# Chunk attention in units of two groups of tokens, and the values of an expert pair as one planned step

## The chip, the cores and the metric

One core of a Trainium2 chip runs the kernel. The metric is device time in microseconds (us), the median of several runs; lower is better. TensorE (PE in the profile) multiplies matrices into PSUM, which has 8 banks of 128 partitions by 512 floats; VectorE (DVE), ScalarE (ACT) and GpSimd (POOL) work on what stands there and in SBUF; SyncE (SP) only issues transfers.

## The reference, cut to what matters

```python
# q, k, v: batch 8, heads 8, sequence 576, head dimension 64
# 1. attention inside chunks of 64 tokens, per head
attn = softmax(q_c @ k_c.T / 8)              # 64 x 64 per chunk and head
x = (attn @ v_c)                             # -> x: 8 x 576 x 512
# 2. four attention experts over x, the two best of them per token
w = softmax over the 2 largest of x @ w_gate
for e in range(4):
    q, k, v = x @ wq[e], x @ wk[e], x @ wv[e]        # 64 wide
    a = softmax(causal(q @ k.T / 8))                 # 576 x 576
    out += (token chose e) * w * ((a @ v) @ wo[e])
```

## The kernel before

The 8 x 576 tokens are cut into 36 groups of 128 tokens (two chunks, all eight heads), g = 0 to 35; four and a half groups make one batch element. Two kinds of work are mixed all along the program.

The **chunk stage** (`stage_a`) takes one group per call. Keys and queries come by DMA into `ks` and `qs`, values into `vs` (256 KB each, three tiles of each kind). TensorE multiplies the scores of 64x64 blocks into two banks (L353, 256 columns of each used). VectorE takes the maximum per bank (L362) and subtracts it (L364), ScalarE takes the exponential (L367), VectorE sums (L369; a 65th column of `e` holds the reference's epsilon) and inverts (L371), and GpSimd multiplies `e` by the inverse into a further tile `en` (L373). TensorE transposes `en` into two banks (L383), ScalarE copies them to `et` (L387), TensorE multiplies with the values (L402), and ScalarE and VectorE write the result as a high and a low part, `xh` and `xl` (L420, L422), which are two fp32r numbers for one fp32.

The **expert stage** runs per batch element: projections of queries and keys for pairs of experts (L451, three products of high and low parts each), values and gate logits (L327), scores (L543), softmax (L553, L561), weights with the gate (L583), transposes (L616, L629 and, on VectorE, L594), values (L648: `values` works on one pair of experts, in two parts of 128 and 448 columns, each with a bank of its own), and the output projection (L676).

What sets the order is a **planner** that runs while the program is built. Every step is added with an engine, a duration, what it depends on, the buffers that it uses, and a key (from the table `KEYS`). `emit` walks through modelled time: whenever an engine is free, the ready step with the lowest key is written out, if its buffers are free. The engines then execute those lists in that fixed order. Each TensorE step has a *form*, after how it splits the array: `full` (128 rows by 128 columns: projections, values and logits, output), `rows` (64 rows by 128 columns: transposes and scores), `cols` (128 by 64: values) and `quarters` (64 by 64: the chunk stage's two products, and the expert scores of the first 64 queries). A step whose form differs from the step before costs `CHANGE` more in the model, and among ready steps whose keys lie within `KEYS["same"]` of the best one of the present form is preferred:

```python
if eng == "PE":
    dur = pe_time(dur + (CHANGE if got.form != form else 0.0), got.share, now)
    form = got.form
```

While TensorE has nothing ready in the first 25 us of modelled time, `emit` writes fillers there, bf16 products of a tile `warm` (L711), to keep the array occupied.

Of the kernel before, what the change touches and what calls it, by code (L numbers as in the profile page):

```python
# [22 lines left out]
NI = 5  # L23
W_VG = E * D + E
# [17 lines left out]
CHANGE = 0.12  # L42
# [13 lines left out]
class Plan:  # L56
# [26 lines left out]
    def emit(self, fill, until):  # L83
# [21 lines left out]
        while left:  # L105
            for eng, heap in avail.items():
# [3 lines left out]
                while heap:  # L110
# [58 lines left out]
def dve_t(n):  # L169
    return 0.075 + 1.04e-3 * n  # L170
# [6 lines left out]
def pool_t(n):  # L177
# [3 lines left out]
KEYS = dict(lead=0.362, a_tr=-3.09, a_av=0.234, a_x=3.312, v=-1.218, vx=2.515, gate=-3.755, q0=1.309, k0=0.512,  # L181
            q1=-0.208, k1=0.186, s0=0.821, s1=1.869, s2=0.46, s3=-0.308, p_soft=0.779, p_tr=0.357, av0=1.956,
            av1=1.843, wo=3.522, vl=5.664, l_qk=8.956, l_v=0.845, l_o=1.057, w=2.854, same=0.118, f_q0=-1.052,
            f_k0=-0.783, f_q1=2.257, f_k1=-1.57, f_v=-0.37, f_vx=3.133, f_gate=1.333, f_s0=0.013, f_s2=-0.982,
            f_av0=0.066, f_av1=0.054, z_q0=-0.132, z_k0=-1.251, z_q1=0.635, z_k1=0.769, z_v=-0.784, z_gate=3.547,
            z_s0=-0.408, z_s2=0.264, z_av0=-1.381, z_av1=0.48, z_wo=1.518, h0=2.856, h1=-0.163, h2=0.071, h3=-0.324)
# [12 lines left out]
def chunked_attention_then_attention_experts(ctx: ExitStack, tc: tile.TileContext, qt, kt, vt, wqk, wvg, wo, out):  # L199
# [12 lines left out]
    q_p = tiles(3, [128, HP, 128], "qs")  # L212
    k_p = tiles(3, [128, HP, 128], "ks")
    vs_p = tiles(3, [128, H, D], "vs")
    e_p = tiles(3, [128, H, 65], "e")
    en_p = tiles(2, [128, DM], "en")
    et_p = tiles(3, [128, 2, 256], "et")
    xc_p = list(zip(tiles(1, [128, KT, 128], "xch", F32R), tiles(1, [128, KT, 128], "xcl", F32R)))
    mx_p = tiles(6, [128, 3, H, 1], "mx")
# [15 lines left out]
    for e in e_p:  # L235
        pool.memset(e[:, :, 64:65], EPS)
# [27 lines left out]
    def load(g):  # L264
        q_s[g], k_s[g], vs_s[g] = Slot(q_p), Slot(k_p), Slot(vs_p)

        def f():
            nc.sync.dma_start(k_s[g].t, kt[g])
            (nc.sync if g else nc.scalar).dma_start(q_s[g].t, qt[g])
        a = add("SP", 1.6, f, uses=[q_s[g], k_s[g]], key=g / 4.5 - 9.0)  # L270
        kq_op[g] = add("dma", 0.0, lambda: None, deps=[a], key=-9.0)
        a = add("SP", 0.8, lambda: nc.sync.dma_start(vs_s[g].t, vt[g]), uses=[vs_s[g]],
                key=KEYS["vl"] * (1.0 / 4.5) + g / 4.5 - 9.0)
        vl_op[g] = add("dma", 0.0, lambda: None, deps=[a], key=-9.0)
# [67 lines left out]
    def stage_a(g):  # L342
        key = (g + 1) / 4.5 - KEYS["lead"] + KEYS.get(f"h{g}", 0.0)
        qs, ks, vs = q_s[g], k_s[g], vs_s[g]
        e, et, mx = Slot(e_p), Slot(et_p), Slot(mx_p)
        bq = [Slot(banks), Slot(banks)]

        def f():
            for hp in range(HP):
                for s in range(2):  # L350
                    for c in range(2):
                        own, cs = slice(64 * s, 64 * s + 64), slice(64 * c, 64 * c + 64)
                        pe.matmul(bq[s].t[cs, 64 * hp:64 * hp + 64], qs.t[own, hp, cs], ks.t[own, hp, cs],  # L353
                                  start=(hp == 0), stop=True, skip_group_check=True)
        o = add("PE", 0.48, f, deps=[kq_op[g]], uses=bq + [qs, ks, e, mx], key=key, share=1.6, form="quarters")
        od = []
        for s in range(2):
            def ps(s=s):
                return bq[s].t[:, 0:256].rearrange("p (h k) -> p h k", h=HP)

            hs = slice(HP * s, HP * s + HP)
            o1 = add("DVE", dve_t(256), lambda ps=ps, hs=hs: dve.tensor_reduce(  # L362
                mx.t[:, 0, hs, 0], ps(), axis=AX.X, op=OP.max), deps=[o], uses=[bq[s], mx], key=key)
            od.append(add("DVE", dve_t(256), lambda ps=ps, hs=hs: dve.tensor_tensor(  # L364
                e.t[:, hs, 0:64], ps(), mx.t[:, 0, hs].to_broadcast([128, HP, 64]), op=OP.subtract),
                deps=[o1], uses=[bq[s], mx, e], key=key))
        o = add("ACT", act_t(512, sbuf=True), lambda: act.activation(e.t[:, :, 0:64], e.t[:, :, 0:64], AF.Exp, scale=0.125), deps=od,  # L367
                uses=[e], key=key)
        o = add("DVE", dve_t(520), lambda: dve.tensor_reduce(mx.t[:, 1, :, 0], e.t, axis=AX.X, op=OP.add),  # L369
                deps=[o], uses=[e, mx], key=key)  # L370
        o = add("DVE", 0.11, lambda: dve.reciprocal(mx.t[:, 2], mx.t[:, 1]), deps=[o], uses=[mx], key=key)  # L371
        en = Slot(en_p)
        o = add("Pool", 1.0, lambda: pool.tensor_tensor(en.t.rearrange("p (h k) -> p h k", h=H), e.t[:, :, 0:64],  # L373
                                                        mx.t[:, 2].to_broadcast([128, H, 64]), op=OP.mult),
                deps=[o], uses=[e, mx, en], key=key)
# [3 lines left out]
        def f():  # L379
            for j in range(HP):  # L380
# [370 lines left out]
```

## Time and profile before

| | us |
|---|---|
| median of 3 runs | 413.78 (412.94 to 414.15) |
| the profiled execution, its own time | 412.04 |
| its span, first to last instruction | 410.3 |
| TensorE busy | 401.0 (98%) |
| ScalarE, VectorE, GpSimd busy | 283.4, 278.6, 176.5 |

The span is what the trace shows; 1.7 us of the profiled execution lie outside it. Matmuls overlap in the array, so TensorE's busy time is not the time that its products need. In a timeline each row is a run of like instructions: start, length, engine, line, operation and tiles; the step from one row's start to the next is what the array was occupied for.

### The profile page before, as it was taken

Reading aid. Unit: us, or ns where it says so; the run is one execution under the profiler, and the core shown is the slowest. Engines: PE = TensorE matmul, PEld = TensorE weight load, DVE = VectorE, ACT = ScalarE, POOL = GpSimd, SP = SyncE. Lnnn points to the kernel's source line nnn. Section 1 sums busy time; section 2 is a strip of 40 time slices with the busy share of each in tenths; the row PEclk is TensorE's granted clock in tenths of the full one; section 3 lists DMA queues with packets and bytes.
Section 4 is the critical chain, followed back from the end, with each engine's and each line's share of the span. In section 5 each row is a group of like instructions: output and inputs, shape, how many; then the busy total and the mean of one; then the engine's idle time right before and its main releaser. Section 6 shows DMA issues by size and latency. Waiting matters only on the chain.

```text
span 410.3 us, 14650 instructions
## 1 busy us (share of the span) xinstructions
PE 401.0 (98%) x5709; PEld 337.4 (82%) x5712; DVE 278.6 (68%) x1021; ACT 283.4 (69%) x949; POOL 176.5 (43%) x359
## 2 busy tenths in 40 slices
PE   6989999999999999999999999999999999999996
PEld 2579999879889899789878889987978989987674
DVE  3779594676884986748669777856576885458642
ACT  4467597797775796957776776898557587578651
POOL 7546039444431149436422207982511214951900
PEclk9999999999999999999999999999999999999999
DMA  8888020104142451204136134201334111000314
GB/s 281 291 289 274 2 78 2 28 3 129 65 119 80 129 190 63 56 33 131 31 112 236 39 132 179 81 2 41 118 104 130 54 66 41 2 2 27 123 60 153
DMA packets 21957, 40.80 MB, mean 99 GB/s; under 512 B 2432, under 2 KB 2432, under 8 KB 21888
## 3 DMA queue, kind: packets, MB, share of 16 engines
q1 hardware_dynamic: 21744, 39.60, 28.9%
q8 instruction: 45, 0.74, 0.8%
q10 hardware_dynamic: 144, 0.26, 0.2%
q14 instruction: 24, 0.20, 0.2%
HBM read 30.42 MB, written 9.44 MB: 97 GB/s over the span
## 4 chain that ended last, share of the span: by engine, by line
PE 92%; DMA 3%; ACT 2%; SPq 1%; issue 1%; DVE 0%; ACTq 0%; DVEq 0%
PE bank L451 26%; PE bank L676 13%; PE bank L327 12%; PE bank L648 11%; PE bank L543 10%; PE bank L616 6%; PE bank L402 4%; PE bank L353 4%; PE bank L383 2%; PE bank L711 2%; DMA at<-in_wqk_dram 2%; DMA qs<-in_qt_dram 1%; ACT at L561 1%; ACT vv L338 1%; ACT et L387 0%
## 5 line engine op out<-in xcount | busy, mean ns | idle before, releaser
L583 POOL TENSOR_SCALAR at<-at,st,gate 64x64 f32<-64x64 f32 (+4 forms) x160 | 95.0, 607 | 51.8 <-DVE st L574 14.1
L561 ACT ACTIVATE at<-at,st 128x192 f32<-128x192 f32 (+4 forms) x160 | 89.1, 563 | 15.1 <-DVE st L553 14.5
L451 PE MATMUL bank<-xh,wqk_hi 128*128 128x320 f32 (+1 forms) x256 | 78.6, 307 | 0.0
L451 PE MATMUL bank<-xl,wqk_hi 128*128 128x320 f32 (+1 forms) x256 | 75.6, 295 | 0.0
L451 PE MATMUL bank<-xh,wqk_lo 128*128 128x320 f32 (+1 forms) x256 | 75.6, 295 | 0.0
L373 POOL TENSOR_TENSOR en<-e,mx 128x512 f32<-128x512 f32 x36 | 37.5, 1045 | 87.3 <-DVE mx L371 54.2
L553 DVE CUSTOM_DVE_ANT_0 at<-bank,mask 64x64 f32<-64x64 f32 (+4 forms) x160 | 60.9, 421 | 11.7 <-PE bank L543 9.1
L629 ACT ACTIVATE aT<-bank 128x128 f32<-128x128 f32 (+2 forms) x256 | 57.2, 364 | 6.0 <-PE bank L616 5.3
L451 PEld LDWEIGHTS bank<-xh,wqk_hi 128*128 128x128 f32 x256 | 48.3, 189 | 2.8 <-DVE st L553 0.7
L451 PEld LDWEIGHTS bank<-xl,wqk_hi 128*128 128x128 f32 x256 | 48.4, 189 | 0.1
L451 PEld LDWEIGHTS bank<-xh,wqk_lo 128*128 128x128 f32 x256 | 48.4, 189 | 0.0
L648 PE MATMUL bank<-aT,vv 128*64 128x448 f32 (+4 forms) x384 | 47.3, 394 | 0.0
L594 DVE STREAM_TRANSPOSE aT<-at 32x96 f32<-32x96 f32 x128 | 34.4, 269 | 14.6 <-PE bank L648 8.5
L648 PEld LDWEIGHTS bank<-aT,vv 128*64 128x64 f32 x384 | 24.9, 136 | 22.1 <-issue 15.1
L362 DVE TENSOR_REDUCE mx<-bank 128x4 f32<-128x256 f32 x72 | 27.7, 413 | 14.9 <-PE bank L353 14.4
L327 PE MATMUL bank<-wvg_hi,xh 128*128 128x260 f32 x128 | 37.8, 295 | 0.0
L327 PE MATMUL bank<-wvg_lo,xh 128*128 128x260 f32 x128 | 36.2, 283 | 0.0
L327 PE MATMUL bank<-wvg_hi,xl 128*128 128x260 f32 x128 | 36.0, 281 | 0.0
L338 ACT ACTIVATE vv<-bank 64x260 f32<-64x260 f32 (+1 forms) x56 | 21.5, 384 | 16.8 <-PE bank L327 16.1
L561 ACT ACTIVATION_READ_ACCUMULATOR at<-at,st 128x1 f32 (+1 forms) x160 | 31.8, 199 | 0.0
L367 ACT ACTIVATE e<-e 128x512 f32<-128x512 f32 x36 | 22.7, 631 | 13.0 <-DVE e L364 11.6
L543 PE MATMUL bank<-kh,qh 64*128 64x288 f32 (+4 forms) x192 | 31.4, 323 | 0.0
(96 smaller groups left out, 869.3 us busy)
## 6 DMA issues: line engine op xcount, KB each, us to landing
ks<-in_kt_dram SPq DMA_DIRECT2D x36, 256.0 KB, 4.1
vs<-in_vt_dram SPq DMA_DIRECT2D x36, 256.0 KB, 3.7
out_dram<-y SPq DMA_DIRECT2D x36, 256.0 KB, 2.0
qs<-in_qt_dram SPq DMA_DIRECT2D x35, 256.0 KB, 4.5
at<-in_wqk_dram SPq DMA_DIRECT2D x4, 256.0 KB, 5.8
at<-in_wvg_dram SPq DMA_DIRECT2D x2, 260.0 KB, 4.1
at<-in_wo_dram SPq DMA_DIRECT2D x2, 256.0 KB, 6.0
qs<-in_qt_dram ACTq DMA_DIRECT2D x1, 256.0 KB, 3.9
```

The lines of the kernel that those rows point to most:

```text
L327: pe.matmul(bk.t[0:rows, :W_VG], xp[:, k, cols], wp[:, k, :], start=(n == 0), stop=(n == 3 * KT - 1))
L362: o1 = add("DVE", dve_t(256), lambda ps=ps, hs=hs: dve.tensor_reduce(mx.t[:, 0, hs, 0], ps(), axis=AX.X, op=OP.max), deps=[o], uses=[bq[s] ...
L373: o = add("Pool", 1.0, lambda: pool.tensor_tensor(en.t.rearrange("p (h k) -> p h k", h=H), e.t[:, :, 0:64], mx.t[:, 2].to_broadcast([128, ...
L451: pe.matmul(bk.t[:, :n_], wp[:, k, 128 * m:128 * m + 128], xp[:, k, c0:c1], start=(n == 0), stop=(n == 3 * KT - 1))
L543: pe.matmul(bks[s].t[:r, :w], q[own, cs], k[own, ks], start=(x == 0), stop=(x == 2))
L553: dve.tensor_tensor_reduce(out=a.t[:r, o_ + ks.start:o_ + ks.stop], in0=bk.t[:r, :w], in1=mask[:r, m0:m0 + w], scale=1.0, scalar=first, op ...
L561: act.activation(af, af, AF.Exp, scale=-1.0, bias=st.t[:r, 0, i, 0:1], accum_out=st.t[:r, 1, i, 0:1])
L583: pool.tensor_scalar(af, af, st.t[:r, 2, i, 0:1], gt.t[:r, i, e:e + 1], op0=OP.mult, op1=OP.mult)
L594: dve.transpose(dst, src)
L629: act.activation(dst, bks[r].t[:, n:n + 64 * m].rearrange("p (j c) -> p j c", j=m), AF.Copy)
L648: pe.matmul(bk.t[64 * s:64 * s + 64, c0 - h0:h1 - h0], vs.t[:, j, 64 * (2 * pair + s):64 * (2 * pair + s) + 64], ts[s].t[:, 448 * j + c0:4 ...
L676: pe.matmul(bk.t, up[:, k, 128 * t:128 * t + 128], wp[:, k, :], start=(n == 0), stop=(n == 5))
```

## The change

The chunk stage works on units. A unit is two neighbouring groups, or the one group that straddles two batch elements; the first unit is split, so that there are 21 units for the 36 groups. Transfers of a unit of two groups are 512 KB, its scores fill two whole banks, and each operation of its softmax is twice as wide. There are two tiles (of two groups) of `qs`, `ks`, `vs`, `e` and `et` each instead of three of one group. `en` is gone: GpSimd multiplies in place in `e`. The column of epsilons moves from `e` to the small tile `mx`, whose sum is taken with an added small reduction. `values` adds one TensorE step for both parts of a pair, which takes both banks at once; the copies stay two. The scores of the first 64 queries run with 128 columns of weights (form `rows`) and only the first 64 rows of the result are read. The planner's `CHANGE` is 0.13, steps that keep the form cost `START[form]`, the tolerance is a number per form, and `KEYS` has new numbers (two of its lines stand here).

```diff
+UNITS = [[9 * n + g for g in u] for n in range(B // 2) for u in ((0, 1), (2, 3), (4,), (5, 6), (7, 8))]
+UNITS[0:1] = [[0], [1]]
-CHANGE = 0.12
+CHANGE = 0.13
+START = {"rows": 0.05, "quarters": 0.05, "cols": 0.1, "full": 0.01}
...
-                    if got is not None and o.key[0] > got.key[0] + KEYS["same"]:
+                    if got is not None and o.key[0] > got.key[0] + KEYS["same_" + form]:
...
-                    dur = pe_time(dur + (CHANGE if got.form != form else 0.0), got.share, now)
+                    dur = pe_time(dur + (CHANGE if got.form != form else START[form]), got.share, now)
...
-KEYS = dict(lead=0.362, a_tr=-3.09, a_av=0.234, a_x=3.312, v=-1.218, vx=2.515, gate=-3.755, q0=1.309, k0=0.512,
+KEYS = dict(lead=0.366, a_tr=-0.329, a_av=0.33, a_x=0.944, v=-2.605, vx=-0.5, gate=0.844, q0=0.676, k0=0.412,
...
-    q_p = tiles(3, [128, HP, 128], "qs")
+    q_p = tiles(2, [128, 2, HP, 128], "qs")
...
-    e_p = tiles(3, [128, H, 65], "e")
-    en_p = tiles(2, [128, DM], "en")
+    e_p = tiles(2, [128, 2 * H, 64], "e")
...
-    def load(g):
-        q_s[g], k_s[g], vs_s[g] = Slot(q_p), Slot(k_p), Slot(vs_p)
+    def load(u):
+        gs = UNITS[u]
+        g, n = gs[0], len(gs)
+        q_s[u], k_s[u], vs_s[u] = Slot(q_p), Slot(k_p), Slot(vs_p)
...
-            for hp in range(HP):
-                for s in range(2):
-                    for c in range(2):
...
+            for n in range(G):
+                for hp in range(HP):
+                    for s in range(2):
+                        for c in range(2):
...
-        o = add("PE", 0.48, f, deps=[kq_op[g]], uses=bq + [qs, ks, e, mx], key=key, share=1.6, form="quarters")
+        o = add("PE", 0.48 * G, f, deps=[kq_op[u]], uses=bq + [qs, ks, e, mx], key=key, share=1.6, form="quarters")
...
-        o = add("DVE", 0.11, lambda: dve.reciprocal(mx.t[:, 2], mx.t[:, 1]), deps=[o], uses=[mx], key=key)
-        en = Slot(en_p)
-        o = add("Pool", 1.0, lambda: pool.tensor_tensor(en.t.rearrange("p (h k) -> p h k", h=H), e.t[:, :, 0:64],
+        o = add("DVE", 0.11, lambda: dve.tensor_reduce(mx.t[:, 2, al, 0], mx.t[:, 1, al], axis=AX.X, op=OP.add),
+                deps=[o], uses=[mx], key=key)
+        o = add("DVE", 0.12, lambda: dve.reciprocal(mx.t[:, 3, al, 0], mx.t[:, 2, al, 0]), deps=[o], uses=[mx], key=key)
+        o = add("Pool", 0.1 + 0.95 * G, lambda: pool.tensor_tensor(
...
-                po = add("PE", 3 * max(0.462e-3 * w, 0.11 if i else 0.055), f, deps=need,
-                         uses=[z] + bks + both, key=key, form="rows" if i else "quarters")
+                po = add("PE", 3 * max(0.462e-3 * w, 0.06), f, deps=need,
+                         uses=[z] + bks + both, key=key, form="rows")
...
-            o = add("PE", 0.22 if h0 == 0 else 2.58, f, deps=deps, uses=[bk, vs] + ts, key=key, form="cols")
+        po = add("PE", 2.8, f, deps=deps, uses=[vs] + ts + [p[2] for p in parts], key=key, form="cols")
```

Where the rows go is seen at three places. On TensorE, in the first quarter of the first batch element: before, the values of one group (L402), two transposes (L383) and two scores (L353) of single groups stand in turn, and the logits and values of x (L327) follow; a line of dots stands for the other rows of the same step.

```order
L402 MATMUL bank_62<-et_83,vs_75 64x64 x2
...
L383 MATMUL bank_61<-ident,en_82 128x64
...
L353 MATMUL bank_64<-ks_74,qs_71 64x64 x2
...
L383 MATMUL bank_63<-ident,en_81 128x64
...
L353 MATMUL bank_61<-ks_72,qs_69 64x64 x2
...
L327 MATMUL bank_66<-wvg_hi,xh_94 128x260
```

Now, at the place that answers to it, transposes of two units stand together (their last row is shown) and run into the expert scores, and then the values of a unit, the scores of the next and the values of another one follow each other (L400, L422 and L367 are the former L383, L402 and L353; L563 is L543, L336 is L327):

```order
L400 MATMUL bank_61<-ident,e_75 128x64
L563 MATMUL bank_63<-kh_92,qh_88 128x64
...
L422 MATMUL bank_68<-et_77,vs_74 64x64 x2
...
L367 MATMUL bank_63<-ks_71,qs_69 64x64 x2
...
L422 MATMUL bank_65<-et_78,vs_73 64x64 x2
...
L336 MATMUL bank_66<-wvg_hi,xch_79 128x260
```

The five changes of form of the first piece have become two in the second (rows to quarters, quarters to full), over more work. Over the whole program the order changes form 232 times before and 152 times now; by the form that is left: full 78 and 60, rows 81 and 52, quarters 55 and 24, cols 18 and 16. The array enters `full` 78 and 60 times. Of fillers there are 40 before and 23 now.

On SyncE, the first transfers. Before, the weights of values and gate (wvg) come second, those of the output (wo) fourth, and the values of a group (vs) after six groups' keys:

```order
L268 DMA ks_72<-in_kt_dram 128x512
L300 DMA at_106<-in_wvg_dram 128x520 x2
L268 DMA ks_73<-in_kt_dram 128x512
L269 DMA qs_70<-in_qt_dram 128x512
L300 DMA at_107<-in_wo_dram 128x512 x2
...
L269 DMA qs_71<-in_qt_dram 128x512
L272 DMA vs_75<-in_vt_dram 128x512
```

Now the two single groups come first, then the weights of queries and keys (wqk, 1 MB), a unit of two groups, the other weights, and the first values:

```order
L277 DMA ks_71<-in_kt_dram 128x512
L277 DMA ks_72<-in_kt_dram 128x512
L278 DMA qs_70<-in_qt_dram 128x512
L309 DMA at_97<-in_wqk_dram 128x512 x2
L309 DMA at_98<-in_wqk_dram 128x512 x2
L277 DMA ks_71<-in_kt_dram 128x2x512
L278 DMA qs_69<-in_qt_dram 128x2x512
L309 DMA at_99<-in_wo_dram 128x512 x2
L309 DMA at_100<-in_wvg_dram 128x520 x2
L277 DMA ks_72<-in_kt_dram 128x512
L278 DMA qs_70<-in_qt_dram 128x512
L281 DMA vs_73<-in_vt_dram 128x512
```

The transfer of wqk has moved from behind 25 transfers of this queue to the fourth place, and five groups' queries and keys are ahead of the first values instead of six.

On VectorE, the chunk softmax at the start of the first batch element. Now the end of two units' chains (a unit of one group on `e_76`, of two on `e_75`) reads so, with a low part of projected keys (L487) between:

```order
L384 TENSOR_REDUCE mx_84<-e_76 128x8
L386 TENSOR_REDUCE mx_84<-mx_84 128x8
L388 RECIPROCAL mx_84<-mx_84 128x8
L384 TENSOR_REDUCE mx_83<-e_75 128x16
L487 TENSOR_TENSOR kl_93<-bank_63,kh_91 128x256
L386 TENSOR_REDUCE mx_83<-mx_83 128x16
L388 RECIPROCAL mx_83<-mx_83 128x16
```

One more small reduction stands in every chain, and in this place the inverse of the double unit is behind a step that waits for ScalarE and TensorE.

## Rows read from the trace of the kernel before

**Rows 1.** Page, part 1: busy us (share of the span), instructions of each engine.
```profile
PE 401.0 (98%) x5709; PEld 337.4 (82%) x5712; DVE 278.6 (68%) x1021; ACT 283.4 (69%) x949; POOL 176.5 (43%) x359
```

**Rows 2.** Page, part 4: the chain that ended last, by engine.
```profile
PE 92%; DMA 3%; ACT 2%; SPq 1%; issue 1%; DVE 0%; ACTq 0%; DVEq 0%
```

**Rows 3.** Windows: length, busy of PE, PEld, DVE, ACT, POOL; clock, DMA share, GB/s.
```profile
0.00:36.20 36.20, 30.78 (x662) 21.26 (x665) 23.72 (x67) 20.31 (x49) 22.54 (x51) 1.00 0.84 287
36.20:398.00 361.80, 361.55 (x5016) 309.45 (x5012) 252.19 (x951) 260.79 (x898) 153.94 (x308) 1.00 0.24 80
```

**Rows 4.** Timeline of TensorE, 380 to 393 us: output projection and transposes in turn.
```profile
380.77 0.39 PE L676 MATMUL bank<-wo_lo,uh 128*128 128x512 f32 x1
381.09 0.90 PE L616 MATMUL bank<-ident,at 64*128 64x64 f32 x22
381.92 0.50 PE L676 MATMUL bank<-wo_hi,uh 128*128 128x512 f32 x1
382.25 0.40 PE L676 MATMUL bank<-wo_hi,ul 128*128 128x512 f32 x1
382.49 0.40 PE L676 MATMUL bank<-wo_lo,uh 128*128 128x512 f32 x1
...
383.51 0.46 PE L616 MATMUL bank<-ident,at 64*128 64x64 f32 x8
383.91 0.50 PE L676 MATMUL bank<-wo_hi,uh 128*128 128x512 f32 x1
...
390.52 1.72 PE L616 MATMUL bank<-ident,at 64*128 64x64 f32 x44
392.17 0.50 PE L676 MATMUL bank<-wo_hi,uh 128*128 128x512 f32 x1
```

**Rows 5.** Timeline of TensorE, 13 to 22 us: chunk scores, and logits and values.
```profile
13.41 0.69 PE L353 MATMUL bank<-ks,qs 64*64 64x64 f32 x32
14.04 0.46 PE L383 MATMUL bank<-ident,en 64*128 64x64 f32 x8
...
19.42 1.16 PE L353 MATMUL bank<-ks,qs 64*64 64x64 f32 x64
20.51 0.39 PE L327 MATMUL bank<-wvg_hi,xh 128*128 128x260 f32 x1
...
22.14 0.50 PE L402 MATMUL bank<-et,vs 64*64 64x64 f32 x17
```

**Rows 6.** Timeline of TensorE: the start, and the first projection of queries.
```profile
1.24 2.74 PE L711 MATMUL bank<-warm 128*128 128x512 bf16 x6 [1.24 <-DVE warm L234]
...
8.50 0.69 PE L353 MATMUL bank<-ks,qs 64*64 64x64 f32 x32 [1.54 <-DMA qs<-in_qt_dram]
9.12 2.55 PE L711 MATMUL bank<-warm 128*128 128x512 bf16 x10
...
36.19 0.39 PE L451 MATMUL bank<-xh,wqk_hi 128*128 128x256 f32 x1
```

**Rows 7.** Windows of 4 us at the start, columns as in rows 3.
```profile
0.00:4.00 4.00, 2.74 (x6) 0.73 (x6) 0.27 (x1) 1.28 (x1) 3.25 (x28) 1.00 0.51 153
4.00:8.00 4.00, 1.82 (x36) 0.87 (x36) 1.79 (x5) 1.90 (x3) 2.93 (x11) 1.00 0.99 358
...
12.00:16.00 4.00, 4.00 (x109) 2.46 (x101) 3.44 (x11) 1.55 (x4) 2.29 (x3) 1.00 0.56 162
```

**Rows 8.** Groups by line: the chunk softmax and the splitting of weights.
```profile
L373 POOL TENSOR_TENSOR en<-e,mx 128x512 f32<-128x512 f32 x36 | 37.5, 1045 | 87.3 <-DVE mx L371 54.2 <-PE bank L543 14.6 <-PE bank L383 11.4
L362 DVE TENSOR_REDUCE mx<-bank 128x4 f32<-128x256 f32 x72 | 27.7, 413 | 14.9 <-PE bank L353 14.4
L369 DVE TENSOR_REDUCE mx<-e 128x8 f32<-128x520 f32 x36 | 24.8, 689 | 7.6 <-ACT e L367 7.1
L367 ACT ACTIVATE e<-e 128x512 f32<-128x512 f32 x36 | 22.7, 631 | 13.0 <-DVE e L364 11.6 <-POOL en L373 1.0
L307 POOL TENSOR_TENSOR wqk_lo<-at,wqk_hi 128x512 fp32r<-128x512 f32 x4 | 5.1, 1288 | 0.4 <-ACT wqk_hi L303 0.4
```

More of the change, by code (lines that the diff above doesn't have):

```diff
@@ L234, in chunked_attention_then_attention_experts @@
     dve.memset(warm, 0.0)
-    for e in e_p:
-        pool.memset(e[:, :, 64:65], EPS)
+    for m in mx_p:
+        pool.memset(m[:, 1, :, 1], EPS)
     ident = sb.tile([128, 128], F32, name="ident")
@@ L377, in stage_a @@
+        o = add("DVE", 0.12, lambda: dve.reciprocal(mx.t[:, 3, al, 0], mx.t[:, 2, al, 0]), deps=[o], uses=[mx], key=key)
+        o = add("Pool", 0.1 + 0.95 * G, lambda: pool.tensor_tensor(
+            e.t[:, al], e.t[:, al], mx.t[:, 3, al, 0:1].to_broadcast([128, 2 * nh, 64]), op=OP.mult),
+            deps=[o], uses=[e, mx], key=key)
         b2 = [Slot(banks), Slot(banks)]
         def f():
-            for j in range(HP):
+            ef = e.t.rearrange("p h k -> p (h k)")
+            for m in range(nh):
@@ L381, in f @@
                 for c in range(2):
                     own = slice(64 * c, 64 * c + 64)
-                    pe.transpose(b2[c].t[:, 64 * j:64 * j + 64], en.t[own, 128 * j:128 * j + 128], ident[own, own])
-        o = add("PE", 0.24, f, deps=[o], uses=[en, et] + b2, key=key, form="rows")
+                    pe.transpose(b2[c].t[:, 64 * m:64 * m + 64], ef[own, 128 * m:128 * m + 128], ident[own, own])
+        o = add("PE", 0.24 * G, f, deps=[o], uses=[e, et] + b2, key=key, form="rows")
         od = []
@@ L396, in f @@
         def f():
[L397 to L405 removed]
+            for n in range(G):
+                for j in range(2):
+                    for c in range(2):
+                        for r in range(2):
+                            for s in range(2):
+                                own, c0 = slice(64 * r, 64 * r + 64), 64 * (2 * G * s + 2 * n + j)
+                                d0 = 128 * (G * j + n) + 64 * c
+                                pe.matmul(bx[r].t[64 * s:64 * s + 64, d0:d0 + 64], vs.t[own, n, 4 * j + 2 * s + c],
+                                          et.t[own, c, c0:c0 + 64],
+                                          start=(n == 0 and j == 0 and c == 0), stop=True, skip_group_check=True)
+        o = add("PE", 0.48 * G, f, deps=od + [vl_op[u]], uses=[et, vs] + bx + ([xc, x_s[b0]] if cut else [x_s[b0]]), key=key,
                 share=1.6, form="quarters")
         n0 = 128 * g - S * b0
[L408 removed]
+        outs = [(x_s[b0], slice(n0, n0 + (64 if cut else 128 * G)), x_part[b0])]
         if cut:
@@ L639, in values, with f @@
         vs = v_s[b]
-        for h0, h1 in ((0, 128), (128, S)):
-            bk = Slot(banks)
-            def f(h0=h0, h1=h1, bk=bk):
+        parts = [(0, 128, Slot(banks)), (128, S, Slot(banks))]
+        def f():
+            for h0, h1, bk in parts:
                 js = [j for j in range(NI) if 128 * j < h1]
@@ L692, in chunked_attention_then_attention_experts @@
     load_w()
-    for g in range(NG):
-        load(g)
-        stage_a(g)
+    for u in range(len(UNITS)):
+        load(u)
+        stage_a(u)
     for b in range(B):
```

96 lines of the change are left out of this document (47 added, 49 removed).

## The prediction

> **What bounds the kernel now.** I read the page's busy times first, then the chain that ended last, then two windows, then TensorE's timeline at its seams and at the start. TensorE is busy 98% of the span, no other engine over 69%, its own overlapping weight loads aside [rows 1], and the chain that ended last is TensorE for 92% and a transfer for 3% [rows 2]. The windows show where the rest lies: from 36.2 to 398 us TensorE is busy 361.55 of 361.80 us at a granted clock of 1.00, and before 36.2 us only 30.78 [rows 3], fillers among them. So a gain must come from TensorE's own time, or from the first 36 us; what VectorE, ScalarE and GpSimd save is hidden.
>
> Busy does not mean that the array does useful work. The timeline shows a price at each change of form [rows 4]. Two products of the output projection in a row start 0.24 apart (382.25 to 382.49). The last one before a transpose holds the array 0.32 (380.77 to 381.09): leaving `full` costs 0.08. The first one after transposes holds it 0.33 (381.92 to 382.25): entering `full` costs 0.09 more. Eight transposes hold it 0.40 (383.51 to 383.91), 44 hold it 1.65 (390.52 to 392.17): 1.25/36 = 0.035 each, so eight should take 0.28, and leaving `rows` costs 0.12. The chunk scores of one group hold it 0.63 (13.41 to 14.04), those of two groups in a row 1.09 (19.42 to 20.51), so a step of `quarters` that follows another saves 2 x 0.63 - 1.09 = 0.17 [rows 5].
>
> **The change part by part.** *Changes of form.* The order has 232 before and 152 now. By the form that is left: 18 fewer from `full`, each with one fewer entry into it, 18 x (0.08 + 0.09) = 3.1 us; 29 fewer from `rows`, 29 x 0.12 = 3.5; 31 fewer from `quarters`, 31 x 0.17 = 5.3; 2 fewer from `cols`, which no row prices, at the neighbours' 0.12, 0.2. Sum 12.1 us. At the cheapest exit for all it is 80 x 0.08 + 18 x 0.09 = 8.0. I take 12.0, since the rows price each form by itself, and keep 8.0 as the other end. The number of products is the same in every kind of step but the fillers, and their shapes are, but for the scores of the first 64 queries. These are 16 pairs x 6 = 96 products with weights 128 instead of 64 wide; transposes with 128-wide weights take 0.035 [rows 4], 3.4 us for 96, and a 64-wide one in `quarters` 0.014 [rows 5], 1.4 us, so at worst +2.0 us. I take 0, because before, too, only two of the four quarters worked on them. It can't gain, since their columns stay.
>
> *The start.* Before, the first projection of queries starts at 36.19 [rows 6]. Until then the order holds the scores of 11 groups and the values of 5 (L402, the same shape; 0.63 each, 10.1 us), the transposes of 8 (0.40 each, 3.2) and four chains of L327 (20.51 to 22.14, 1.63 each, 6.5 [rows 5]): 19.8 us. So 16.4 us are lost to waits and fillers. Now the first L327 (L336 in the new text) has ahead of it two single scores in a row (1.09), a double one (1.09), a single one (0.63), two transposes (0.68) and two values (1.26): 4.75 us. When it can start hangs on the first values (`vs`): keys and queries of five groups (2.62 MB), wqk 1.05, wo 0.52, wvg 0.53 and `vs` 0.26 are 4.98 MB. The transfers move 0.61 MB by 4 us (153 GB/s) and then 358 GB/s [rows 7]; the 162 of 12 to 16 us is a queue that waits for free tiles, which the new order needs up to there only for the scores of the first two units. That gives 4 + 4.37/0.358 = 16.2 us. A transfer lands later than its bytes: the second queries, 1.58 MB down the line, should land at 4 + 0.97/0.358 = 6.7 and are waited for until 8.50 [rows 6], 1.8 late. So `vs` is there at 18.0, its product takes 0.63, the split into high and low two operations on each of two engines, 1.2 us if each takes as long as the reduction of the same 128x256 bank, 0.41 [rows 8]. L336 starts at 19.9, and 15.1 us are lost. GpSimd is close behind: five splits of weights at 1.29 and two multiplications at 1.05 stand ahead of the two for wvg, 11.1 us in all [rows 8], which from about 7 us end at 18.1. The start thus gains 16.4 - 15.1 = 1.3 us. Ends: at 287 GB/s, the mean of the first 36.2 us [rows 3], `vs` is 3.0 later, a loss of 1.7; without the 1.8 of lateness, a gain of 3.1.
>
> *What may wait anew.* A double unit's softmax is longer. From the reductions of 256 and 520 elements (413 and 689 ns), one element costs 1.05 ns; at twice the width the two maxima, two subtractions, the sum and GpSimd's multiplication take 0.68 x 4 + 1.22 + 2.05 us, and the exponential about 1.1 for 0.63 [rows 8]. With two small operations that is 7.5 us where a single group took 4.2. Counted in the new order with the prices above, at least 10 us of TensorE's work stand between a unit's scores and its transposes once the first batch element is under way, so it is covered, unless VectorE comes late. At the start it comes late once: the inverse of the first double unit stands behind a low part that waits for a projection. `values` needs two free banks at once; before, its two parts followed each other in all but two of 16 places, so it adds little. Two tiles instead of three hold four groups instead of three; a unit's keys may be issued when the unit before the last has its scores, and by the prices above the order has 15 us or more between the two after the first batch element. The 21 added reductions, at most 0.41 each, and the saved ones of 69 fewer instructions in the chunk softmax, lie beside TensorE. For all of this I put 1.5 us, 0.1 for each of the 15 double units; in the trace before, TensorE's idle after 36.2 us is 0.25 us in all [rows 3], which is the low end, and 3 us, twice my value, is the high one. The tail, 36 products of the output projection behind the last values, is the same.
>
> *Sum.* -12.0 - 1.3 + 1.5 = -11.8 us. The profiled execution took 412.04, 1.7 of it outside the span; it becomes 400.2. The median of the runs is 413.78, 1.74 above it; the forecast for the median is 402.0. The ends of the terms give -12.1 - 3.1 + 0.2 = -15.0 (398.8) and -8.0 + 2.0 + 1.7 + 3.0 = -1.3 (412.5); all at their bad end together is unlikely, so the forecast's own range is 399 to 406.
>
> **The rivals.** *The clock falls at the start.* 23 fillers stand where 40 stood, and by the sum above TensorE pauses some 3 us before the first transposes and again before the first values. For it: pauses are longer than before. Against it: through the pause of 1.54 us before 8.50 and the fillers around it the granted clock stays 1.00 [rows 6, 7]. The six fillers of the very start take 2.74/6 = 0.46 each, ten later ones 2.55/10 = 0.26 [rows 6]; a stretch at half speed costs nearly its length again. If the first values, logits and one projection run so, 3 us of work cost 3 us more: 405.
> The Trainium skill, "TensorE: Matmul & The Clock Gate", section "HAM oscillation — how this bites in real kernels", speaks for this rival: there, short bursts of matmuls with a wait for a transfer between them lose the full clock, and each burst starts cold. No row of this trace shows such a fall.
>
> *Part of the gain comes back as waits.* The planner's durations for the doubled operations are its own; where VectorE or ScalarE runs a little late in each operation, the transposes, or the product that needs their copies `et` some 2.5 us later, come late. For it: VectorE and ScalarE are busy 68% and 69% [rows 1], in some stretches more. Against it: the list before ran with next to no idle [rows 3] by the same rules. At 0.5 us for each of 15 double units it costs 7.5 instead of 1.5: 408.
>
> *Slower than before.* One mechanism: the longer chain of a double unit is not covered. Its place is the transposes (L400) behind GpSimd's multiplication, its price what the chain is longer, 3.3 us, for 15 units, at most 50 us. It decides once TensorE stands for 0.8 us more at each of them than I put, 11.8/15. For it: GpSimd's largest waits are just there, 54.2 us for VectorE's inverse [rows 8], so the chain has no reserve of its own. Against it: TensorE did not wait for it [rows 3], and over 10 us of work cover it. At 1.1 us more for each: 418.
>
> **How the numbers follow.** The forecast has 0.72, the clock 0.10, the waits 0.12, slower 0.06. About 0.3% (1.2 us) is what a measurement of this kernel can tell from no change. The forecast and the clock are faster, the waits for two thirds (the rest of it, 0.04, within 0.3%); so faster 0.90, same 0.04, slower 0.06. The range of 8 in 10 goes from 398.5, just under the good ends of the terms, to 409, past the third case's time.
>
> **What would show it.** Right: TensorE's products per line unchanged but the fillers; 36 chunk scores in 21 steps; the same 0.08 to 0.17 us at each seam and 80 fewer seams; the first L336 near 20 us and the first projection right behind; busy all through from there. Wrong: idle of TensorE before L400 or L422 that VectorE, GpSimd or a transfer of `vs` ends, which speaks for the second or third rival; fillers or first products at twice their time after 8 us, for the first; or seams that stay although the order has fewer.

## The result, and the profile after

The changed kernel takes 408.34 us (median of 13 runs, 406.16 to 412.12), the kernel before on the same chip 412.37 (13 runs, 410.64 to 415.22): ratio 0.991, 95% interval 0.9887 to 0.9933. That is 4.0 us less where 11.8 were forecast: the direction was right, the size a third. The profiled execution took 410.81 us, 2.5 above its own median, against 412.04 before, so this pair of traces differs by only 1.2 us. Here and below, a ratio counts the runs within 1.5% of the fastest of their kernel.

The page of the changed kernel, part 1 and the first line of part 4, answers to [rows 1, 2]:

```profile
PE 395.1 (97%) x5693; PEld 337.9 (83%) x5695; DVE 272.1 (67%) x922; ACT 273.9 (67%) x874; POOL 173.1 (42%) x345
...
PE 93%; issue 2%; DMA 1%; POOL 1%; DVE 1%; ACT 1%; SPq 0%; POOLq 0%; DVEq 0%; ACTq 0%
```

TensorE is busy 5.9 us less, yet the span shrank by 1.4: it now stands still more. "Issue", time in which an engine waits for nothing that the profile shows, is 2% of the chain. Windows of three stages (columns as in [rows 3]) show where, first of the changed kernel:

```profile
0.00:25.00 25.00, 19.79 (x291) 12.89 (x294) 12.23 (x31) 11.50 (x23) 16.63 (x47) 1.00 0.90 309
25.00:62.00 37.00, 33.48 (x717) 31.55 (x716) 24.37 (x76) 21.58 (x61) 14.77 (x28) 0.95 0.39 130
62.00:398.00 336.00, 334.79 (x4661) 288.21 (x4660) 233.40 (x814) 238.98 (x787) 141.75 (x272) 1.00 0.24 79
```

and of the kernel before:

```profile
25.00:62.00 37.00, 36.49 (x567) 33.58 (x569) 27.74 (x106) 27.23 (x86) 14.65 (x26) 1.00 0.44 147
62.00:398.00 336.00, 335.75 (x4708) 285.12 (x4707) 232.67 (x870) 242.57 (x837) 147.40 (x290) 1.00 0.24 80
```

From 25 to 62 us TensorE is idle 3.52 us where it was 0.51, and the granted clock is 0.95 instead of 1.00. After 62 us it is idle 1.21 us against 0.25. TensorE's timeline shows the idle pieces (start, length, ..., count, idle before it and what ended it):

```profile
30.38 0.69 PE L422 MATMUL bank<-et,vs 64*64 64x64 f32 x32
30.89 1.11 PE L367 MATMUL bank<-ks,qs 64*64 64x64 f32 x64
31.83 0.52 PE L422 MATMUL bank<-et,vs 64*64 64x64 f32 x20
33.05 0.91 PE L422 MATMUL bank<-et,vs 64*64 64x64 f32 x44 [0.71 <-issue]
...
37.56 0.28 PE L471 MATMUL bank<-xl,wqk_hi 128*128 128x256 f32 x1
39.69 0.39 PE L471 MATMUL bank<-xh,wqk_lo 128*128 128x256 f32 x1 [1.85 <-issue]
...
42.49 0.47 PE L471 MATMUL bank<-xl,wqk_hi 128*128 128x320 f32 x1
42.76 0.47 PE L471 MATMUL bank<-xh,wqk_lo 128*128 128x320 f32 x1
...
60.97 0.56 PE L367 MATMUL bank<-ks,qs 64*64 64x64 f32 x20 [0.94 <-issue]
...
95.56 0.36 PE L471 MATMUL bank<-xh,wqk_hi 128*128 128x256 f32 x1 [0.74 <-ACT aT L649]
```

The pauses stand inside steps: at 31.83 within one step of 64 products, at 37.56 within one chain of a projection, whose operands and bank are all there. A third, of 0.94, is in the chunk scores at 60.0 us. After the pause of 1.85 the clock is at its lower level (1.2 GHz) from 40.79 to 44.20 us, by the trace's record of the grant: products of 320 columns then start 0.27 apart, elsewhere 0.15. Half of 3.41 us, 1.7 us, is lost so. (This record begins at 16.9 us here; before it, the column of the windows shows 1.00 for want of a record, and the products run at half speed.)

The pair adds up as follows (working in the section on the prediction; the last row is what the others leave of the measured 1.2, and no row of a trace shows it by itself):

| term | forecast | in this pair |
|---|---|---|
| changes of form | -12.0 | -9.3 |
| scores of the first 64 queries | 0 | +2.2 |
| pauses, 25 to 62 us | in no term | +3.0 |
| half clock behind them | a rival | +1.7 |
| idle after 62 us | +1.5 | +1.0 |
| start, and what is left over | -1.3 | +0.2 |
| sum | -11.8 | -1.2 |

### The profile page after: what moved, and what is told of

Its sections match the earlier page's. It is cut to its first block, busy times and chain, and to the rows that moved or that the text cites. A ratio compares the mean times of both kernels' runs of the same rounds, so it can differ in the third digit from the quotient of the medians.

```text
span 408.9 us, 14272 instructions
## 1 busy us (share of the span) xinstructions
PE 395.1 (97%) x5693; PEld 337.9 (83%) x5695; DVE 272.1 (67%) x922; ACT 273.9 (67%) x874; POOL 173.1 (42%) x345
## 4 chain that ended last, share of the span: by engine, by line
PE 93%; issue 2%; DMA 1%; POOL 1%; DVE 1%; ACT 1%; SPq 0%; POOLq 0%; DVEq 0%; ACTq 0%
PE bank L471 27%; PE bank L696 13%; PE bank L336 13%; PE bank L668 11%; PE bank L563 11%; PE bank L636 6%; PE bank L422 5%; PE bank L367 4%; PE bank L400 2%; DMA at<-in_wqk_dram 1%; POOL wqk_lo L316 1%; PE bank L731 1%; DVE aT L614 1%; POOL e L389 0%; ACT aT L649 0%
## 5 line engine op out<-in xcount | busy, mean ns | idle before, releaser
L581 ACT ACTIVATE at<-at,st 64x64 f32<-64x64 f32 (+4 forms) x160 | 90.0, 569 | 17.3 <-DVE st L573 16.4
L389 POOL TENSOR_TENSOR e<-e,mx 128x1024 f32<-128x1024 f32 (+1 forms) x21 | 35.0, 1669 | 46.9 <-PE bank L636 21.4
L668 PEld LDWEIGHTS bank<-aT,vv 128*64 128x64 f32 x384 | 25.0, 137 | 21.3 <-issue 15.8
L336 PE MATMUL bank<-wvg_hi,xh 128*128 128x260 f32 x128 | 37.4, 292 | 0.0
L336 PE MATMUL bank<-wvg_lo,xh 128*128 128x260 f32 x128 | 36.2, 283 | 0.0
L336 PE MATMUL bank<-wvg_hi,xl 128*128 128x260 f32 x128 | 36.0, 281 | 0.0
L513 POOL TENSOR_TENSOR gs<-vv,gs 128x20 f32<-128x20 f32 x8 | 2.5, 308 | 75.0 <-DVE gs L507 75.0
L563 PE MATMUL bank<-kh,qh 64*128 64x64 f32 (+3 forms) x192 | 33.6, 336 | 0.0
L376 DVE TENSOR_REDUCE mx<-bank 128x8 f32<-128x512 f32 (+1 forms) x42 | 24.4, 607 | 10.8 <-PE bank L367 10.8
```

The lines of the kernel that those rows point to most:

```text
L336: pe.matmul(bk.t[0:rows, :W_VG], xp[:, k, cols], wp[:, k, :], start=(n == 0), stop=(n == 3 * KT - 1))
L389: o = add("Pool", 0.1 + 0.95 * G, lambda: pool.tensor_tensor(e.t[:, al], e.t[:, al], mx.t[:, 3, al, 0:1].to_broadcast([128, 2 * nh, 64]), ...
L563: pe.matmul(bks[s].t[:, :w], q[own, cs], k[own, ks], start=(x == 0), stop=(x == 2))
L581: act.activation(af, af, AF.Exp, scale=-1.0, bias=st.t[:r, 0, i, 0:1], accum_out=st.t[:r, 1, i, 0:1])
L668: pe.matmul(bk.t[64 * s:64 * s + 64, c0 - h0:h1 - h0], vs.t[:, j, 64 * (2 * pair + s):64 * (2 * pair + s) + 64], ts[s].t[:, 448 * j + c0:4 ...
```

## The experiments

The theory after this result: TensorE's own instructions come too late. The page lists them as a queue of their own:

```profile
q8 instruction: 45, 0.74, 0.8%
```

That is 45 packets of 16 KB for 11,388 instructions (products and weight loads), 253 to a packet. In the trace a packet moves about once per 256 instructions of TensorE, and the version with some 6,900 more of them (chunk scores four times over, below) has 72. Rivals: a disturbance of one execution; data that come late; the start.

**The changed kernel again, twice** (no edit).

> The changed kernel once more, nothing else. Theory (TensorE's instructions arrive late where the program's order makes it use them up fast, so the pauses belong to the program): TensorE again stands still for 0.5 to 2 us, released by nothing that the trace shows, near 32, 37 and 60 us, the first full clock again comes later than 12 us, and the time is 406 to 411 us. Rival (a disturbance of the one profiled execution): no such pause of over 0.3 us between 30 and 62 us, no half clock after 20 us, and a span near 404 us.

> The changed kernel once more, for a comparison on one chip with the next two: 406.5 to 409 us, with the pauses near 32, 37 and 59 us in the profiled execution.

Measured 407.73 us (6 runs, ratio to before 0.9914, 0.9886 to 0.9942) and 407.78 (7 runs, 0.9895, 0.9873 to 0.9917). The pauses recur in both profiles: 0.45, 1.57 and 0.69 us at 32.1, 37.4 and 59.3, and 0.42, 2.66 and 1.93 at 31.6, 36.8 and 59.8, with half clock from 39.5 and 39.8 us, and none behind the 1.93. In all three profiles they stand behind the same instructions of TensorE, the 949th, 1204th and 1964th product or weight load of the trace. They belong to the program; their length varies. Of the 26 timed executions of the changed kernel 12 had a mean granted clock of 0.997 or more (median 407.6), 14 less (409.1); of 60 of the kernel before, 53 and 7 (411.4 and 413.0). So with the full clock on both sides the change is still worth less than 4 us: half clock alone is not what is missing.

**Short loads**, in both kernels.

```diff
+            m, p = (2, 128) if u == 3 else (n, 128 if u < 4 else 8)
-            nc.sync.dma_start(k_s[u].t[:, 0:n], src(kt))
+            nc.sync.dma_start(k_s[u].t[0:p, 0:m], src(kt, m)[0:p])
```

(likewise for queries and values; in the kernel before, from the sixth group on)

> The changed kernel with the same order; from the fifth unit on each load of keys, queries and values moves 8 of its 128 partitions (the others keep what an earlier unit left there), so the transfer engines are nearly idle from about 25 us on. Theory that TensorE's own instructions wait behind these loads: the pause near 37 us (1.85 us) and the half clock behind it (1.7 us) go, those near 32 and 60 us (0.7 and 0.9), which had little or no traffic when their instructions were fetched, stay or shrink a little: 3.5 to 4.5 us less than the changed kernel, near 404. Theory that only the dense run of small products uses the instructions up: all three pauses stay, 407 to 409. Theory that late data is behind the missing gain: TensorE's waits for loads go, but the trace shows none after 20 us, so nothing changes.

> The kernel before with the same cut: from the sixth group on each load moves 8 of 128 partitions, order unchanged. If instructions wait behind loads: the pauses at 22.3, 25.0, 29.6 and 31.8 us (0.88, 0.15, 0.20, 0.16) go, 1.4 us less, near 411.0; with the changed kernel cut in the same way the difference of the two then shows what the change is worth without this collision, which the seams and the wider scores alone put at 10.5 - 2.2 = 8.3 us. If loads play no part: 412.4 as before, and the difference of the two stays near 4.

Measured 407.61 us (6 runs, 0.9904, 0.9879 to 0.9929) and 409.67 (7 runs, 0.9960, 0.9939 to 0.9981). Windows of the changed kernel with short loads, then of the kernel before with them:

```profile
25.00:62.00 37.00, 35.39 (x748) 33.66 (x747) 27.39 (x82) 23.25 (x65) 16.75 (x30) 1.00 0.08 25
```

```profile
25.00:62.00 37.00, 37.00 (x544) 34.71 (x544) 27.08 (x105) 28.11 (x86) 17.04 (x31) 1.00 0.09 29
```

The mechanism is as expected: in the changed kernel the pause at 37 us and the half clock behind it are gone, while one of 0.45 in the values and one of 1.15 in the scores stay; in the kernel before every pause of this stage is gone, and by the ratio it is 1.6 us faster, about the 1.4 expected. So instructions do wait behind loads, but that is only part. The changed kernel's time was missed: it gained nothing measurable. In the one execution profiled its start was worse (half clock until 14.06 and, behind a pause of 1.15 in the first values, again from 20.88 to 24.30 us); whether the others lost the same isn't known. The two kernels came to 2.1 us of each other, not 8.3. Loads alone don't explain the missing gain.

**Chunk scores four times over**, one execution: what dense rows of small products do by themselves.

```diff
-            for n in range(G):
+            for n in 4 * list(range(G)):
```

> The changed kernel with every chunk-score step issued four times over (each bank is written again with the same numbers), order otherwise the same: a double unit has 256 products of 64x64 in a row, 512 instructions of TensorE. At the 0.0145 us that one such product takes in a dense row, the added 36 x 96 products are 50 us: 459 us if nothing else holds them. Theory (TensorE's instructions come in blocks of 256, about 2.7 us from the moment one is asked for, so that a row of small products uses them up faster than they come): nearly every double unit shows one or two pauses of 0.5 to 1.5 us inside the step, with no data on the move as well, and the time is 470 to 490 us. Rival (pauses come only where loads are on the move): pauses in a few units, 459 to 464 us.

Measured 505.41 us, beyond the theory's range. The group of the chunk scores, with its idle time and what ended it:

```profile
L367 PE MATMUL bank<-ks,qs 64*64 64x64 f32 x4608 | 80.6, 223 | 40.2 <-issue 39.1 <-DMA qs<-in_qt_dram 1.1
```

39.1 us of pauses in these steps, against 0.9 in the changed kernel; 50 us of products and 38 more of pauses leave some 9 of the 97 added. This trace also has more half clock (from 10.8 to 17.6 us, and three stretches of 3.41 us later), but that it is just these 9 isn't shown. One place on TensorE's timeline:

```profile
401.35 3.49 PE L367 MATMUL bank<-ks,qs 64*64 64x64 f32 x223
406.12 0.73 PE L367 MATMUL bank<-ks,qs 64*64 64x64 f32 x33 [1.29 <-issue]
...
407.11 1.11 PE L367 MATMUL bank<-ks,qs 64*64 64x64 f32 x62
409.93 2.09 PE L367 MATMUL bank<-ks,qs 64*64 64x64 f32 x128 [1.72 <-issue]
413.42 1.26 PE L367 MATMUL bank<-ks,qs 64*64 64x64 f32 x66 [1.39 <-issue]
```

Between the last two pauses lie 128 products, a product and a weight load each: 256 instructions, one packet. From 409.93 to 413.42 are 3.5 us where 128 products need 1.9. The transfers from 400.8 to 406.4 us, around the first of these pauses:

```profile
DMA packets 1, 0.02 MB, mean 3 GB/s; under 512 B 0, under 2 KB 0, under 8 KB 0
## 3 DMA queue, kind: packets, MB, share of 16 engines
q8 instruction: 1, 0.02, 1.2%
```

Nothing moves but the instructions, and TensorE pauses all the same. This settles the rival that pauses come only with loads: a dense row alone makes them. In long rows 256 instructions take 3.5 to 4.0 us from the end of one pause to the end of the next (once 5.4, with a load on the move), not the 2.7 of the expectation, which is one reason why its range failed.

The packets' own times fit in every trace. The one in that window begins at 403.41 and has landed at 404.53, and TensorE goes on at 406.12; the pause of 1.85 in the changed kernel ends at 39.69 after a packet from 37.27 to 38.23. In all 14 traces together TensorE has 74 idle times of over 0.3 us that end after 17 us and not at a filler. Two end with a transfer of queries; the other 72 all end 1.2 to 1.6 us after a packet of instructions has landed. Four of them the profile puts down to ScalarE's copy, the one of 0.74 at 94.8 us above among them. They too stand at a multiple of about 256 instructions from the others, and with short loads this one isn't there, so they are most likely pauses for instructions as well.

**First 64 queries in quarters again**, order kept.

```diff
-                    cs = slice(q0(i), q0(i) + 128)
+                    cs = slice(q0(i), q0(i) + r)
-                            pe.matmul(bks[s].t[:, :w], ...
+                            pe.matmul(bks[s].t[:r, :w], ...
```

> The changed kernel with the same order, but the scores of the first 64 queries with 64-wide weights again (the form of quarters). Theory (prices as in the trace before): 96 products at 27.5 ns instead of 54.1, 2.5 us less, against 19 more changes of form, 16 of them out of quarters at 0.17 and 3 out of rows at 0.12, 3.1 us more: +0.5 us, no measurable difference; the six products of one such step take 0.17 instead of 0.32. Rival (the wider weights cost nothing, as the prediction had it): the steps take as long as now and the 19 changes make it about 3 us slower. Rival (a change of form costs half of what the rows say): about 1 us faster.

Measured 408.01 us (5 runs, 0.9898, 0.9861 to 0.9935): no measurable difference, as the first theory had it; a step of six products takes 0.20 us in most places instead of 0.36. The traces tell more: from the 49th product of the output projection to the last, a stretch in which neither has a pause of over 0.3 us, the changed kernel takes 201.2 us and this version 200.4, with 9 more changes of form. There the wider weights cost 0.8 us more than the changes that they avoid.

**The loads of wo later** (l_o=9.0 for 2.056, run twice), and **with the values earlier** (l_o=6.0, vl=4.0).

> The changed kernel with the key of the loads of wo raised from 2.056 to 9, so that 0.52 MB and two splits on GpSimd leave the start; the list of instructions changes with it. Theory that the start is bound by transfers up to the first values: these come 0.52/0.358 = 1.5 us sooner, the first L336 and the first projection of queries by as much, and the time is 1 to 2 us lower, near 406.5. Rival (the start is bound elsewhere, or what is won is lost to the pauses that follow): no measurable difference.

> The version with the loads of wo later, again: by the first runs 406.2, so 1 to 2 us below the changed kernel on the same chip; if the first result was chance, within 0.5 us of it. The pause before 37 us stays small (0.2 before, 1.6 to 1.9 in the changed kernel), the one near 55 us (1.8) is there.

> The changed kernel with the key of the loads of wo at 6 and that of the values at 4 instead of 6.37: wo leaves the start, and the first values are asked for ahead of later keys and queries. By the transfers alone the first values land 1.5 us sooner for wo and up to 2.9 us sooner for one double unit's keys and queries that they pass: the first L336 between 17 and 19.5 us instead of 21.1, the time 2 to 4 us lower, 404 to 406. Rival (the softmax of the double unit that was passed is then late instead): the first L336 is earlier, but the 20th chunk step is not, and the time is within 1 us of the changed kernel.

Measured 406.16 (6 runs, 0.9879, 0.9853 to 0.9905), 407.06 (6 runs, 0.9885, 0.9863 to 0.9906) and 408.01 us (6 runs, 0.9907, 0.9881 to 0.9933). In the first profile the first L336 starts at 19.96 where the changed kernel had it at 21.32, as the theory said, and the pause near 36 us is 0.2. The second time it is 20.65, after a pause of 2.98 at 16.5 us, and the time is 0.7 us below the changed kernel's on the same chip, between the two expectations; so the gain is not reliable. The third version has its first L336 at 20.05, outside the 17 to 19.5 expected, and its time is the rival's; it has pauses of 1.66, 0.40, 1.29 and 1.83 us, the last with half clock behind it. The start is worth about 1 us, and even that is not shown: the interval of the first version overlaps the changed kernel's.

**Fewer changes, longer rows**: three edits of the planner (0.32 us for a step of the first 64 queries, instructions that come 256 at a time, keys chosen anew).

```diff
+                        if used % 256 == 0:
+                            end = max(end, block[used // 256])
+                            block.append(end + (5.5 if end < loading else 3.7))
```

> The changed kernel with three changes of the planner: it counts the scores of the first 64 queries at 0.32 us a step instead of 0.18, it holds TensorE where its instructions would not be there yet (256 at a time, each 3.7 us after the one before was begun, 5.5 while a load is on the move), and its keys are chosen anew under these prices. Its list has 20 fewer changes of form than the changed kernel (124 against 144 by the planner's count), and rows of 5 to 8 groups in quarters in each batch element. Theory that the price of a form change and the supply of instructions are what decides: 20 x 0.13 = 2.6 us less than the version with late wo, and pauses of 1 to 2 us only behind the rows of 7 and 8 groups: 401 to 404 us. Rival (the longer rows cost more in pauses, and in half clock behind them, than the seams save): pauses of over 0.5 us in most batch elements and 406 to 409 us.

Measured 413.68 us (12 runs, 1.0052, 1.0028 to 1.0077): 0.5% slower than the kernel before although it has the fewest changes of form of all. The rival's mechanism holds, and the time lies even beyond its 406 to 409. What TensorE waited for:

```profile
PE bank L381 <- issue: 5.7, 4, 2.4
PE bank L436 <- issue: 4.3, 4, 1.6
...
PE bank L485 <- issue: 1.4, 1, 1.4
```

11.4 us of pauses, most of them in the chunk scores (L381 here) and values (L436), where 20 fewer changes of form were to save 2.6.

**Shorter rows, more changes**: two sets of keys, rows of at most 4 groups (but one of 6 in the first), wo late.

> The changed kernel with other keys (wo late, and chosen so that rows of steps in quarters stay short): at most 4 groups in a row, but for one row of 6, where the changed kernel has one of 8 and four of 5; 153 changes of form by the planner's count where the changed kernel has 144. Theory (the missing part of the gain is TensorE waiting for its own instructions behind long rows, and half clock behind such waits): no pause over 0.5 us released by nothing after 25 us, but for one behind the row of 6; full clock from there; the 9 changes cost 1.1 us, the pauses and the half clock give back 3 to 4: 403 to 405.5 us. Rival (each change of form counts and the pauses don't): 1 us slower than the changed kernel, 408 to 410.

> Another choice of keys of the same kind: no row of more than 4 groups, 161 changes of form by the planner's count, 17 more than in the changed kernel. Theory (as for the other one): no pause over 0.5 us after 25 us, full clock from there; 17 changes cost 2.0 us, pauses and half clock give back 3 to 4: 404 to 406.5 us. Rival (changes of form alone): 2 us slower than the changed kernel, 409 to 411.

Measured 410.51 us (12 runs, 10 of them in the ratio, 0.9947, 0.9917 to 0.9976) and 406.78 (6 runs, 0.9886, 0.9850 to 0.9922). The second is 0.3 us above its expectation, with 17 more changes and yet no slower than the changed kernel; its windows:

```profile
25.00:54.00 29.00, 29.00 (x608) 27.03 (x606) 24.99 (x78) 21.20 (x58) 12.94 (x21) 1.00 0.47 157
54.00:62.00 8.00, 6.36 (x179) 6.05 (x172) 6.94 (x20) 4.80 (x11) 6.96 (x12) 1.00 0.86 277
```

Without a long row there is no idle time from 25 to 54 us. But the bound of 4 groups was wrong: a pause of 2.04 us stands at 16.8, and pauses of 1.65 and 1.50 at 55.9 and 88.2, that at 55.9 behind three steps with loads on the move (0.86 of the transfer engines busy). The first version missed its expectation by 5 us: its profile, 2 us below its median, has pauses of 0.72 and 1.00 and one of 2.44 in a chain of logits at 246 us, where 2.57 MB move in 9 us, and what its other executions lost isn't known. A rule that bounds the row alone is therefore not enough; the loads near it count as well.

## Why the prediction was wrong, step by step

Three steps failed. The part on what may wait anew priced waits for operands and buffers alone; that TensorE waits for its own instructions had no term, and took 3.0 us between 25 and 62 us in the pair of traces, with 1.7 of half clock behind it. The scores of the first 64 queries were put at 0 and cost 2.2. The changes of form were put at 12.0, and 9.3 came. Of the start's 1.3 nothing was seen.

**What bounds the kernel** was read rightly: the gain came from TensorE's time, and what the other engines saved is hidden.

**Changes of form.** The mechanism was right; the price of quarters and the number of changes that count were off. Full and rows cost what they did [rows 4]; two seams of the changed kernel:

```profile
376.92 0.40 PE L696 MATMUL bank<-wo_lo,uh 128*128 128x512 f32 x1
377.25 0.91 PE L636 MATMUL bank<-ident,at 64*128 64x64 f32 x22
...
381.37 0.50 PE L696 MATMUL bank<-wo_hi,uh 128*128 128x512 f32 x1
381.71 0.39 PE L696 MATMUL bank<-wo_hi,ul 128*128 128x512 f32 x1
```

0.33 to leave and 0.34 for the first, as before. Quarters were taken at 0.17 from one pair of steps at the start [rows 5]. Over the trace of before after 25 us, 33 single steps without idle time that another form follows take 0.616 in the mean and 14 that quarters follow 0.514: 0.10. In the changed kernel 14 double steps that another form follows take 1.064 and 10 that quarters follow 0.977: 0.09. One place of it, where a single step of 32 is followed by a double one of 64 and that by the output projection:

```profile
130.12 0.69 PE L422 MATMUL bank<-et,vs 64*64 64x64 f32 x32
130.64 1.11 PE L367 MATMUL bank<-ks,qs 64*64 64x64 f32 x64
131.68 0.50 PE L696 MATMUL bank<-wo_hi,uh 128*128 128x512 f32 x1
```

0.52 and 1.04. With 31 x 0.10 = 3.1 for 5.3 the sum is 9.9. And 5 of the 80 changes lie beside fillers, where TensorE waits anyway: 0.6 less, 9.3.

**Scores of the first 64 queries**, taken at 0 with a worst case of 2.0: this step failed. One step of the kernel before, then one of the changed kernel:

```profile
123.07 0.24 PE L543 MATMUL bank<-kh,qh 64*64 64x64 f32 x2
123.15 0.22 PE L543 MATMUL bank<-kl,qh 64*64 64x64 f32 x2
...
123.36 0.69 PE L402 MATMUL bank<-et,vs 64*64 64x64 f32 x32
```

```profile
124.19 0.28 PE L563 MATMUL bank<-kh,qh 64*128 64x64 f32 x2
124.30 0.28 PE L563 MATMUL bank<-kl,qh 64*128 64x64 f32 x2
...
124.67 0.50 PE L696 MATMUL bank<-wo_hi,uh 128*128 128x512 f32 x1
```

A pair takes 0.11 to 0.13 instead of 0.08. From its first product to the next step a step took 0.24 in the mean of 16 and takes 0.38 now: 16 x 0.14 = 2.2 us. That only two quarters worked before did not make the wider weights free.

Both terms together, -7.1 us, can be tested apart from the start and the pauses: the stretch from the 49th to the last of the 216 products of the output projection is half of the program, has 34 of the 80 changes and half of these scores, and no more than 0.2 us of idle time. It went from 204.9 to 201.2 us, 3.7 less; the same prices give 3.1. In three profiles of the changed kernel it is 201.2 each time. So this part of the gain is there, and what is missing was lost in the first half of the program.

**The start** gave nothing. TensorE's timeline of the changed kernel, and two rows of GpSimd's:

```profile
8.56 0.58 PE L731 MATMUL bank<-warm 128*128 128x512 bf16 x1 [1.49 <-DVE e L378]
...
12.62 0.69 PE L400 MATMUL bank<-ident,e 64*128 64x64 f32 x8 [0.49 <-POOL e L389]
...
14.24 1.98 PE L367 MATMUL bank<-ks,qs 64*64 64x64 f32 x64
...
20.30 0.69 PE L422 MATMUL bank<-et,vs 64*64 64x64 f32 x32
...
21.32 0.47 PE L336 MATMUL bank<-wvg_hi,xh 128*128 128x260 f32 x1
```

```profile
7.83 3.73 POOL L316 TENSOR_TENSOR wqk_lo<-at,wqk_hi 128x512 fp32r<-128x512 f32 x3 [2.63 <-ACT wqk_hi L312]
11.52 2.05 POOL L389 TENSOR_TENSOR e<-e,mx 128x512 f32<-128x512 f32 x2
```

The first values were forecast for 18.0 and started at 18.64, with a pause for instructions of 0.45 inside them; the second follow at 20.30, and the first L336 starts at 21.32 (20.5 to 21.3 in three profiles) instead of 19.9. Three splits on GpSimd hold the first softmax up, and at half clock the double step takes 1.98 instead of 1.04. The clock explains a part: it was full from 16.9 us in this profile and for good from 12.2 and 12.5 in the other two, whose first values start 0.8 to 0.9 sooner, but the pause in them is 1.10 in one, and their first L336 is 0.2 and 0.8 sooner. In the kernel before it was full from 4.1 us.

**New waits** were sized well by luck: 1.0 us after 62 us for 1.5, but 0.74 of it is the idle time at 94.8, most likely one more pause for instructions, so waits of the kind that was forecast are some 0.2 us more than before. The longer chain of the double unit is covered, as argued: after the start TensorE never waits for GpSimd's multiplication.

**The rivals.** The clock rival happened, for another reason than the waits of the start: the full clock came late, and fell again behind a pause. The rule of the Trainium skill cited with it, that bursts with waits between them lose the full clock, agrees with the trace in this place: 0.5 granted from 40.79 to 44.20 us after 1.85 us of standing still. It does not hold behind each pause: after 1.93 us at 59.8 in the third profile the clock stayed full. Waits for other engines and the slower case did not occur. None of the cases named what took the largest part, TensorE pausing for its own instructions, although the trace before has such a pause too (0.88 us at 22.6 us, put down to "issue").

What stays open: how long the pauses are in the executions without a trace, which make the median, since only one execution of each version has one; why the clock fell behind some pauses and not behind others; and what made the first version with short rows slow.

## What to carry to other kernels

Grouping steps of one form saves about 0.1 us of TensorE at each seam, but where the products are so small that 128 of them pass in under 2 us, a row of more than about that many made TensorE wait for instructions here, at 0.3 to 3.0 us a pause in these orders; with loads on the move shorter rows did, too. So count instructions along the new order as well as seams, keep small products apart by large ones, and above all where loads come in bursts. A wider operand in a cheaper form is not free: time it from a row of the same shape.

## What the hardware showed that was not expected

- TensorE's instructions come in packets of 16 KB, 256 at a time, and in a row of 64x64 products no faster than one packet in 3.5 to 4.0 us, 27 to 31 ns for a product with its weight load, where such products start 15 ns apart in short rows. The Trainium skill, "Runtime: NRT & Kernel Launch", section "Instruction fetch mechanics", has blocks of 256 instructions fetched while the current one runs, the cost mostly hidden. The block agrees (253 to a packet here). That it is hidden does not hold in these rows: 39.1 us of pauses in the run with repeated scores.
- With loads on the move the pause grows: 1.6 to 2.7 us near 37 us in the three profiles of the changed kernel, none there with short loads.
- Of 14 pauses of 1.5 to 2.7 us after 25 us (all traces but that of the repeated scores), 7 had a stretch of 3.41 us at half clock behind them, at a cost of 1.7 us, and 7 none: 2.42 and 1.93 left the clock full, 1.57 did not.
- A pair of products with 128-wide weights and 64 columns starts 0.11 to 0.13 us after the one before, with 64-wide weights 0.06 to 0.08.
